# Dummy products in front of three groups, a later start for a weight conversion, and a new order of groups

## The chip, the cores and the metric

The kernel runs on one NeuronCore of a Trainium2 chip. The metric is the device time of one execution in microseconds (us); lower is better. The engines are called as the profile calls them: PE is TensorE (PEld its weight loads), DVE is VectorE, ACT is ScalarE, POOL is GpSimd, and SP issues nearly all transfers.

## What is computed

Three layers run one after another: a delta-rule attention with a 48 x 48 state for each of 4 x 8 heads over 768 tokens, a product layer, and a layer of soft routing over 32 slots.

```python
for t in range(S):                                   # 768 tokens, state 48x48 for each head
    y[:, :, t] = einsum('bhd,bhde->bhe', q[:, :, t], state)
    v_old = einsum('bhde,bhd->bhe', state, kt)       # kt: normalised key
    state = state + bt * outer(kt, vt - v_old)
x = y.transpose(0, 2, 1, 3).reshape(3072, 384)
h = ((x @ w1) * (x @ w2)) @ w3                        # 384 -> 1024 -> 1024
x = h @ w_out                                         # 1024 -> 384
logits = x @ phi                                      # 384 -> 32 slots
d = softmax(logits over tokens); c = softmax(logits over slots)
slot_in = d.T @ x
slot_out[e] = relu(slot_in[e] @ w1[e]) @ w2[e]        # 8 experts, 4 slots each
return c @ slot_out
```

The weights of the second layer (w1, w2, w3, w_out, phi) arrive as 64-bit floats and are turned into 32-bit floats on the chip.

## The kernel before

The tokens of each head are cut into 24 pieces of 32 (`chain0` to `chain23`), and two pieces make one of 12 chunks. In one piece the recurrence is a small triangular system: `G` products (line 476) give the inner products of keys and queries, `solve0` to `solve5` (lines 503 to 618, DVE and POOL) invert the triangles of four pieces at once, and the `chain` steps carry the state on. The steps of chain n are `pre` (POOL, line 644), `ks` (PE, line 658, then a subtraction on DVE), `vv` (PE, line 669, four copies on ACT), `yy` (PE, line 679, one copy on ACT), for odd n `ss` (PE, line 689, the state), and `xt` (line 701: three transposes on PE, then a copy on ACT and a subtraction on DVE). `xt` fills the tile xT of its chunk.

Once both pieces of chunk c have gone through `xt`, `prod` c runs: eight steps of 18 products of 128 x 256 (line 754), 144 for a chunk, each step with an ACT copy (line 758) and a DVE multiplication (line 763). `gtr` c turns the result around (line 771) and `post` c makes logits, softmax and the weighted sums (lines 778 to 857). The whole of w3, w_out and phi is folded into one matrix `wphi`, which `post` 0 is the first to need. So the second layer's conversions come before: `w12.0` to `w12.7` convert w1 and w2 (lines 353 to 355), and the 32 steps labelled `w3` convert w_out (eight, products on lines 370 and 375) and w3 (24, products on lines 391, 395 and 404). A step of `w3` issues a raw load on SP, six element-wise operations on DVE, ACT and POOL (lines 328 to 337), a store to DRAM on SP, and PE products with copies. Four raw tiles (`hold`) take turns.

The order is written by times. `when` and `spread` put every step in a list with a time in units of chunks, plus the `SHIFT` of its label; `spread(TW0, TW1, ...)` places the 32 steps of `w3`. `run` sorts the list and traces the steps in that order. The tile scheduler then fixes each engine's instruction order: of the instructions that it takes to be ready, the one traced first goes first. Each engine then works through its own list in order. PSUM tiles are dealt from pairs of banks by tag: `at` (chain, joins of the solves, most G products), `tr` (conversions, `gtr`, `post`) and `ab` (`prod`). `xt` of chain n takes `at` for n < `NXT` and `tr` from there on.

After the last chunk a tail computes the experts and the output. There, `warm` issues runs of eight or two 128 x 128 bf16 products into spare columns of the bank `sacc` (line 211), whose results nothing reads.

Of the kernel before, what the change touches and what calls it, by code (L numbers as in the profile page):

```python
# [11 lines left out]
BF16 = mybir.dt.bfloat16  # L12
# [30 lines left out]
DR = 0.223  # L43
NU = 2
NUG = 10
TW0 = 0.51
TW1 = 0.8
CL = 1.003
NW = 2
# [7 lines left out]
W1 = -0.8  # L57
WG = (0, 3, 7)
PV = (0, 1, 2, 3)
P0 = (-8.466, -1.081, -0.8, -0.6)  # L60
NR12 = 2
NSPLIT = 0
NXT = 12
GL = (0.35, 0.659, 0.85, 1.06)
NX = 6
NO = 8
GX = 3.912
LT = 1.693
LTS = 0.467
JAT = (1, 2, 3)  # L70
PP = 16
LAST = 1
EA = 11.832
JO = (-0.7, 0.007, 0.216)
G1 = -0.439
S1 = -0.015
S2 = 0.006

# [21 lines left out]
SB = -0.192  # L100


SHIFT = {'w3': -0.052, 'solve4': 0.109, 'gtr3': 0.007, 'solve3': 0.315, 'prod11': 0.006, 'chain20': 0.021, 'gtr8': -0.158, 'chain17': -0.056, 'gtr6': 0.158, 'post0': -0.014, 'chain19': 0.048, 'gtr10': 0.016, 'back0': 0.257, 'gtr2': -0.016, 'chain13': -0.173, 'gtr9': 0.002, 'back1': 0.128, 'post10': -0.015, 'chain23': -0.207, 'gtr0': 0.04, 'G8': 0.031, 'gtr11': -0.005, 'chain8': -0.107, 'gtr5': 0.116, 'chain5': -0.257, 'prod7': -0.026, 'chain10': -0.118, 'v6': 0.004, 'chain15': 0.036, 'prod6': 0.084, 'chain12': -0.053, 'v19': 0.5, 'G16': -0.125, 'post8': 0.057, 'prod10': 0.031, 'chain1': -0.277, 'v10': -0.038, 'chain4': 0.021, 'chain22': -0.057, 'G12': -0.152, 'prod9': -0.214, 'G22': 0.034, 'P0': -0.102, 'prod8': -0.053, 'v14': 0.146, 'solve2': 0.227, 'load7': 0.158, 'load6': -0.201, 'v13': -0.51, 'gtr1': 0.069, 'solve0': -0.184, 'post9': -0.107, 'load10': 0.047, 'G14': 0.047, 'chain18': -0.04, 'chain16': -0.002, 'chain2': -0.275, 'post4': -0.112, 'load2': -0.042, 'chain21': -0.033, 'v21': -0.195, 'chain6': 0.289, 'w12': 0.061, 'load0': 0.01, 'load1': -0.089, 'v20': -0.163}

TRACE = None

# [24 lines left out]
def kern(ctx, tc, kq, vt, kt, bl, w12, w3, wo, phi, w1e, w2e, consts, out):  # L131
    nc = tc.nc
    V, A, G, T = nc.vector, nc.scalar, nc.gpsimd, nc.tensor
# [61 lines left out]
    sv = px.tile([128, 4, H * D], F32, name="sv")  # L195
    sacc = [ps.tile([128, 512], F32, name=f"sacc{i}") for i in range(2)]
# [8 lines left out]
    zw = cs[:, C_ID:C_ID + 64].bitcast(BF16)  # L205
# [14 lines left out]
    def before(p):  # L220

        return p - 4 if p < HP else p - 5
# [19 lines left out]
    def lab(l):  # L242
        if TRACE:
            TRACE(nc, l)

    def when(t, *steps, label="when"):

        t += SHIFT.get(label.split(".")[0], 0.0)
        for f in steps:
            events.append((t, len(events), f, label))  # L250

    def spread(lo, hi, steps, label="-"):
        for i, f in enumerate(steps):
            when(lo + (hi - lo) * (i + 0.5) / len(steps), f, label=f"{label}.{i}")

    def run():
        for t, _, f, label in sorted(events, key=lambda z: z[:2]):
            lab(label)
            f()
        events.clear()  # L260
# [103 lines left out]
    def wo_steps():  # L364
        def cv(g):
            w = to_f32(raw_load(wo[:, g, :], DM, f"wo{g}"), DM, f"wo{g}")
            SP.dma_start(out=wod[:, g, :], in_=w)
            p = tr(f"wot{g}")
            for k in range(3):
                T.transpose(p[:, k * 128:(k + 1) * 128], w[:, k * 128:(k + 1) * 128], ident)  # L370
            wt = pl["stage"].tile([128, 384], F32, tag="cf", name=f"woT{g}", bufs=2)[:, 0:DM]
            A.copy(wt, p[:, 0:DM])
            p = tr(f"wm{g}")
            for k in range(3):
                T.matmul(p[:, 0:32], lhsT=wt[:, k * 128:(k + 1) * 128], rhs=phis[:, k, :], start=(k == 0), stop=(k == 2))
            V.tensor_copy(mwp[:, g, :], p[:, 0:32])

        return [lambda g=g: cv(g) for g in range(8)]
# [79 lines left out]
    def g_step(n, hs, which="gp"):  # L458

        s, n4 = divmod(n, 4)  # L460
        if n4 == 0 and "g" in which and hs[0] == 0:
            Dg[s] = pk.tile([128, 32, 32], F32, tag="L", name=f"dg{s}", bufs=NL)
        t = kl_of(n // 2)
        k = [(3, 3), (5, 1)][n % 2]

        span = {"gp": [((3, 7), (0, 4)), ((5, 7), (0, 2))], "g": [((3, 4), (3, 4)), ((5, 6), (1, 2))],
                "p": [((4, 7), (0, 3)), ((6, 7), (0, 1))]}[which][n % 2]
        nb = span[0][1] - span[0][0]
        p = (ab if n // 4 == 1 else at)(f"{which}{n}_{hs[0]}")
        gp = p[:, 0:len(hs) * nb * 32].rearrange("p (h k i) -> p h k i", h=len(hs), k=nb)  # L470
        for h in hs:
            for b in range(4):
                r, kc, j = srow(b), kcol(h, b), b // 2
                lo, hi = span[j]
                slots = slice(lo, hi) if j == 0 else slice(hi - 1, lo - 1 if lo else None, -1)
                m = T.matmul(gp[trow(n, b), h - hs[0]], lhsT=t[r, k[j], kc], rhs=t[r, slots, kc], start=True, stop=True)  # L476
        last_g[:] = [m]
        blocks = {}
        if "g" in which:
            blocks["g"] = 0  # L480
        if "p" in which:
            blocks["p"] = o = len(which) - 1
            blocks["x"] = o + 1
        g_evac(n, hs, gp, blocks, n < PP and n not in PV)

    def g_parts(p):

        h = H // 2
        return [lambda: g_step(2 * p, range(h)), lambda: g_step(2 * p, range(h, H)), lambda: g_step(2 * p + 1, range(H))]
# [145 lines left out]
    def chain_steps(n):  # L635
# [59 lines left out]
        def xt():  # L695
            ys = st["y"]
            if t2 == 0:
                xT[c] = [pl["xt"].tile([128, 3, 2, 128], F32R, tag="xT", name=f"xT{c}_{i}", bufs=4) for i in range(2)]
            p = (at if n < NXT else tr)(f"xp{n}")
            for k in range(3):  # L700
# [164 lines left out]
    def zeros(t=held4):  # L865
        V.memset(t[0:64, 5, :], 0.0)
        V.memset(t[64:128, 1, :], 0.0)

    def first():
        V.memset(sv[:, 0, :], 0.0)  # L870
        G.memset(sv[:, 1:4, :], 0.0)
        for t in kls:
            zeros(t)
        for p in sacc:
            T.matmul(p[:, 0:384], lhsT=sv[:, 0, 0:128], rhs=sv[:, 0, :], start=True, stop=False, skip_group_check=True)

    def behind0(f):

        def g():
            with tc.issue_after(ends[0].ins):  # L880
                f()
        return g

    def behind_x(f):

        def g():
            with tc.issue_after(solved[0].ins):
                f()
        return g

    def behind_w12(f, k):

        def g():
            with tc.issue_after(last_v[k].ins if k >= 0 else ends[0].ins):
                f()
        return g
# [43 lines left out]
    when(-8.87, lambda: load_kk(0), lambda: load(2), lambda: load_b(1))  # L940
    when(-8.86, lambda: load(3), gate.clear)
    when(-8.95, first)
    when(-8.95, lambda: A.activation(out=nid, in_=ident, func=AF.Copy, scale=-1.0))
    for i in range(4):
# [7 lines left out]
    for n in range(4):  # L952
        for hs in [range(H)] if n % 2 else [range(H // 2), range(H // 2, H)]:
            f = lambda n=n, hs=hs: g_step(n, hs, "p")
            when(P0[n], f if P0[n] < -8.6 else behind_x(f), label="P0")
    spread(W0, W1, [behind_w12(f, i - AHEAD) for i, f in enumerate(w12s)], "w12")
    when(-1.0, lambda: SP.dma_start(out=phis, in_=phi))
    when(-0.75, open_main)
    spread(TW0, TW1, [behind_w12(f, 7) for f in wo_steps() + w3_steps()], "w3")

    def ct(x):

        return x - CL - DR * x / NCH
# [10 lines left out]
    for p in range(3, NCH):  # L974
# [3 lines left out]
        else:  # L978
            t = ct(before(p) + 1.01) + max(0, *[SHIFT.get(f"chain{2 * before(p) + i}", 0) for i in range(2)])
        if p > 3:  # L980
            when(t, lambda p=p: load(p))
        ready[p] = HT + 0.01 if p == HP else before(p) + 1.06
    for s in range(1, NSS):
        for p in range(2 * s, 2 * s + 2):
            if s == 1:
                for i, g in enumerate(g_parts(p)):
                    when((G1, G2)[p % 2] + 0.001 * i, behind0(g), label=f"G{2 * p}")
            else:
# [11 lines left out]
    for c in range(NCH):  # L1000
        a, b, p = main_steps(c)
        spread(c, c + 1, a, f"prod{c}")

        late = LT + LTS * c
        t, w = (c + 0.25, 1.0) if late < c + 0.25 else (max(late, c + 0.7), 0.4)
# [31 lines left out]
    when(ct(2 * NSS - 2 + SB) + 0.01, early_solve, label="T.early")  # L1037
    when(GX, early_gates, label="T.early")
    when(ct(NCH - 0.1), close_att, label="close")
    eep = {}  # L1040
    for s0 in (0, 2):
        when(EA + 0.01 * s0, lambda s0=s0: eep.update(a=halves(s0)), label="T.eeA")
        for t in range(4):
            when(EA + 0.01 * s0, lambda s0=s0, t=t: expand(eep["a"], t, pl["ee"][:, s0:s0 + 2]), label="T.eeA")
    run()
    mn_stack.close()
    ws_stack.close()
# [72 lines left out]
    for hf in range(2):  # L1120
        p = ab(f"h1p{hf}")
        for f in range(8):
            q = 32 * (f % 4)
            T.matmul(p[q:q + 32], lhsT=uT[:, f % 4, f // 4, :], rhs=w3s[hf][f],
                     start=(f < 4), stop=(f >= 4), skip_group_check=True)
# [19 lines left out]
    for f in range(8):  # L1145
        q = 32 * (f % 4)
        m = T.matmul(p[q:q + 32, 0:384], lhsT=h1T[:, f, :], rhs=wos[:, f, :], start=(f < 4), stop=(f >= 4),
                     skip_group_check=True)
# [205 lines left out]
```

## Time and profile before

| what | us |
|---|---|
| median of 3 runs | 622.87 |
| lowest and highest run | 621.13, 624.06 |
| the profiled execution's own time | 618.74 |
| its span, first to last instruction | 616.9 |
| PE busy in the span | 565.4 |
| DVE, ACT, POOL busy | 393.9, 281.8, 126.8 |

The profile is of one execution. Its time is its span and 1.84 us around it, and lies 4.13 us under the median of the runs. A busy PE is not a PE at its best: the small products of the chain overlap each other, and a product takes longer in stretches where the granted clock is 0.50 (1.2 GHz) than where it is 1.00 (2.4 GHz). The mean granted clock is 0.950.

### The profile page before, as it was taken

The numbers are of one execution on the slowest core, as the hardware profiler recorded it, in microseconds if no ns is written. First come the engines' busy times: TensorE is split into PE (matmuls) and PEld (weight loads), VectorE is DVE, ScalarE is ACT, GpSimd is POOL, SyncE is SP. The second block draws the span as 40 slices with busy tenths as digits, with TensorE's granted clock in tenths as the row PEclk, the third lists the DMA queues.
The fourth block names the chain that finished last, engine by engine and source line by source line (L and its number), as shares of the span: only waits on it lengthen the run. The fifth ranks groups of instructions, "written<-read, shape, count | busy, mean of one in ns | idle before, by whom it ended". The sixth has DMA issues, their size and how long they took to land.

```text
span 616.9 us, 26156 instructions
## 1 busy us (share of the span) xinstructions
PE 565.4 (92%) x11506; PEld 461.7 (75%) x11508; DVE 393.9 (64%) x1275; ACT 281.8 (46%) x709; POOL 126.8 (21%) x191
## 2 busy tenths in 40 slices
PE   4679879997989999999989999999989999999996
PEld 3355558895767778779879897988988888885364
DVE  3998977976699649831499827987991313224124
ACT  1047874454457444554425445435544354323023
POOL 1111274342454250122300103013011000000100
PEclk9988977798799999989989999999999999999997
DMA  6974181057548622401304040312425132688818
GB/s 181 299 165 183 29 241 55 3 156 245 157 144 243 169 72 68 101 15 39 79 3 100 16 101 16 103 59 81 141 79 202 53 109 95 229 271 321 332 67 278
DMA packets 36945, 81.73 MB, mean 132 GB/s; under 512 B 4352, under 2 KB 17792, under 8 KB 35584
## 3 DMA queue, kind: packets, MB, share of 16 engines
q1 hardware_dynamic: 36576, 79.61, 42.8%
q8 instruction: 90, 1.47, 1.0%
q10 hardware_dynamic: 256, 0.46, 0.3%
q14 instruction: 23, 0.19, 0.1%
HBM read 69.57 MB, written 10.49 MB: 130 GB/s over the span
## 4 chain that ended last, share of the span: by engine, by line
PE 39%; DVE 20%; POOL 4%; issue 2%; ACT 1%; DMA 1%; POOLq 0%; ACTq 0%; DVEq 0%
PE ab L754 18%; DVE tmp L562 5%; DVE xl L565 5%; PE gp L771 2%; PE sacc L1199 2%; PE hp L1178 2%; PE gp L476 2%; PE yp L679 2%; PE vp L669 2%; PE lp L778 1%; PE sacc L689 1%; PE ks L658 1%; DVE xl L540 1%; DVE gl L503 1%; DVE gT L763 1%
## 5 line engine op out<-in xcount | busy, mean ns | idle before, releaser
L754 PE MATMUL ab<-xT,wsl 128*128 128x256 f32 x1728 | 244.8, 294 | 0.6 <-DVE gx L763 0.5
L754 PEld LDWEIGHTS ab<-xT,wsl 128*128 128x128 f32 x1728 | 220.1, 195 | 11.3 <-issue 5.6
L763 DVE TENSOR_TENSOR gT<-ab,bs 128x256 f32<-128x256 f32 x84 | 34.9, 418 | 86.5 <-ACT bs L758 85.7
L758 ACT COPY bs<-ab 128x256 f32<-128x256 f32 x96 | 35.6, 372 | 78.0 <-PE ab L754 77.3
L644 POOL TENSOR_TENSOR v<-v,nnT 128x384 f32<-128x384 f32 x24 | 21.6, 898 | 188.1 <-DMA v<-vt 90.3
L633 ACT COPY sv<-vp 32x384 f32<-32x384 f32 x96 | 45.2, 471 | 11.2 <-PE vp L669 9.5
L565 DVE TENSOR_TENSOR xl<-xl,tmp 128x84 f32<-128x84 f32 (+35 forms) x220 | 48.9, 252 | 0.8
L562 DVE TENSOR_TENSOR tmp<-xl 128x84 f32<-128x84 f32 (+35 forms) x220 | 49.1, 253 | 0.5
L476 PE MATMUL gp<-kl 48*32 48x128 f32 (+1 forms) x1152 | 39.7, 272 | 7.0 <-ACT kl L456 4.5
L337 POOL TENSOR_TENSOR hold<-hold 128x384 f32<-128x384 f32 (+1 forms) x32 | 31.9, 999 | 45.3 <-DVE hold L334 24.5
L476 PEld LDWEIGHTS gp<-kl 48*32 48x32 f32 x1152 | 28.4, 118 | 15.0 <-ACT kl L456 6.0
L772 ACT COPY gtok<-gp 128x512 f32<-128x512 f32 x48 | 28.2, 587 | 18.2 <-PE gp L771 17.4
L456 ACT COPY kl<-gp 32x256 f32<-32x256 f32 x72 | 26.2, 364 | 22.0 <-DVE kl L441 21.1
L771 PE MATMUL gp<-cs,gT 128*128 128x128 f32 x168 | 27.4, 282 | 2.9 <-DVE gT L763 2.7
L330 DVE SCALAR_TENSOR_TENSOR hold<-hold 128x384 int32<-128x384 int32 (+1 forms) x32 | 23.7, 741 | 7.5 <-ACT hold L329 6.9
L329 ACT ACTIVATE hold<-hold,cs 128x384 int32<-128x384 int32 (+1 forms) x32 | 18.5, 589 | 18.4 <-DVE hold L328 17.2
L658 PE MATMUL ks<-sv,kl 48*32 48x48 f32 (+2 forms) x1344 | 23.9, 210 | 1.7 <-issue 1.1
L669 PEld LDWEIGHTS vp<-v,w 32*32 32x32 f32 x1536 | 19.8, 108 | 7.1 <-issue 4.0
L669 PE MATMUL vp<-v,w 32*32 32x48 f32 x1536 | 24.4, 207 | 0.6 <-DVE w L618 0.6
L658 PEld LDWEIGHTS ks<-sv,kl 48*32 48x32 f32 (+2 forms) x1344 | 19.6, 111 | 6.2 <-issue 2.9
L679 PE MATMUL yp<-sv,kl 112*32 112x48 f32 (+2 forms) x1408 | 24.2, 208 | 0.0
L771 PEld LDWEIGHTS gp<-cs,gT 128*128 128x128 f32 x168 | 19.6, 143 | 5.9 <-issue 2.8
(252 smaller groups left out, 960.0 us busy)
## 6 DMA issues: line engine op xcount, KB each, us to landing
hold<-w SPq DMA_DIRECT2D x16, 384.0 KB, 3.7
v<-vt SPq DMA_DIRECT2D x24, 192.0 KB, 2.5
kk<-kt SPq DMA_DIRECT2D x12, 384.0 KB, 6.8
kl<-kq SPq DMA_DIRECT2D x9, 512.0 KB, 7.1
kl<-w1e SPq DMA_DIRECT2D x6, 768.0 KB, 5.3
unitg<-w2e SPq DMA_DIRECT2D x6, 768.0 KB, 4.6
kl<-kq SPq DMA_DIRECT2D x9, 384.0 KB, 4.9
hold<-wo SPq DMA_DIRECT2D x8, 384.0 KB, 5.9
```

Source lines behind the costliest of these rows:

```text
L337: last_m.append(E.tensor_tensor(out=w, in0=m, in1=w, op=ALU.mult))
L476: m = T.matmul(gp[trow(n, b), h - hs[0]], lhsT=t[r, k[j], kc], rhs=t[r, slots, kc], start=True, stop=True)
L562: V.tensor_tensor(out=tmp[:, 0:n, lo:hi], in0=x[:, j + 1:32, j:j + 1].to_broadcast([128, n, hi - lo]), in1=x[:, j:j + 1, lo:hi].to_broadca ...
L565: V.tensor_tensor(out=x[:, j + 1:32, lo:hi], in0=x[:, j + 1:32, lo:hi], in1=tmp[:, 0:n, lo:hi], op=ALU.add)
L633: A.copy(o, i)
L658: T.matmul(kp[o, h], lhsT=kl[r, (5, 1)[b // 2] if t2 else 3, kcol(h, b)], rhs=sv[r, b, h * D:(h + 1) * D], start=True, stop=True, tile_pos ...
L669: T.matmul(p[o, h * D:(h + 1) * D], lhsT=w[o, 8 * n4 + h, :], rhs=r[o, h, :], start=True, stop=True, tile_position=(o.start, o.start))
L679: T.matmul(p[qrow(b), h * D:(h + 1) * D], lhsT=kl[r, (6, 0)[b // 2] if t2 else (4, 2)[b // 2], kcol(h, b)], rhs=sv[r, b, h * D:(h + 1) * D ...
L754: T.matmul(o, lhsT=w[:, m, k], rhs=x[:, k], start=(n == 0), stop=(n == 8))
L758: A.copy(bs, p[:, 256:512])
L763: V.tensor_tensor(out=gt, in0=p[:, 0:256], in1=bs, op=ALU.mult)
L771: T.transpose(p[:, t * 256 + i * 128:t * 256 + (i + 1) * 128], gt[:, t * 128:(t + 1) * 128], ident)
```

## The change

It has three parts.

1. A table `FILL` names three steps: `chain5.2` (the `vv` of chain 5), `w12.7` (the eighth conversion of w1 and w2) and `prod0.2` (the third step of prod 0). In front of each, `run` traces 16, 8 and 12 products of 128 x 128 bf16 into the spare columns of `sacc[0]`. Each is tied by order alone, with no semaphore, behind the PE instruction traced just before it. One more product of zeros at the start gives these columns a value.
2. `TW0` goes from 0.51 to 0.719, so that the 32 steps of `w3` begin 0.2 chunks later in the list and end where they ended.
3. Other constants move single groups: `solve3`, `chain13`, `chain7`, `G14`, `gtr4`, `prod5`, all `gtr` and `post` after chunk 0 (`LTS`), the early load of some expert weights (`GX`), and the first P0 and G4 steps by 0.05 and 0.004. `NXT` goes from 12 to 5.

Sorted, the two lists hold the same 641 steps. The first difference is at place 110. In the old list `load_b(2)` stood after `w3.0`, the load of v for chain 4 after `w3.1`, `chain3.0` after `w3.5`, `prod0.4` after `w3.11` and `chain3.1` after `w3.14`; in the new one these five stand ahead of all of `w3`. `chain3.2` goes from after `w3.23` to after `w3.2`, and `prod0.5` from after `w3.24` to after `w3.7`. `chain3.3` and all that follows stands behind all of `w3` in both. From there the lists agree until `gtr1.0`, `chain6.1` and `chain7.0`, which are places 203 to 209.

```diff
-TW0 = 0.51
+TW0 = 0.719
-P0 = (-8.466, -1.081, -0.8, -0.6)
+P0 = (-8.516, -1.081, -0.8, -0.6)
-NXT = 12
+NXT = 5
-GX = 3.912
+GX = 3.873
-LTS = 0.467
+LTS = 0.444
-G1 = -0.439
+G1 = -0.435
...
-SHIFT = {... 'solve3': 0.315, ... 'chain13': -0.173, ... 'G14': 0.047, ...}
+SHIFT = {... 'solve3': 0.26, ... 'chain13': -0.29, ... 'G14': 0.016, ..., 'chain7': 0.052, 'gtr4': -0.15, 'prod5': 0.158}
+FILL = {'chain5.2': 4, 'w12.7': 2, 'prod0.2': 3}
...
         for t, _, f, label in sorted(events, key=lambda z: z[:2]):
+            for _ in range(4 * FILL.get(label, 0)):
+                tc.keep_in_program_order(T.matmul(sacc[0][:, 384:512], lhsT=zw, rhs=zw, start=False, stop=False,
+                                                  skip_group_check=True))
             lab(label)
             f()
...
             T.matmul(p[:, 0:384], lhsT=sv[:, 0, 0:128], rhs=sv[:, 0, :], start=True, stop=False, skip_group_check=True)
+        zero = sv[:, 0, 0:128].bitcast(BF16)
+        T.matmul(sacc[0][:, 384:512], lhsT=zero[:, 0:128], rhs=zero[:, 0:128], start=False, stop=False, skip_group_check=True)
```

## Rows read from the trace of the kernel before

**Rows 1.** The page: busy us by engine (share of the span), instructions.
```profile
PE 565.4 (92%) x11506; PEld 461.7 (75%) x11508; DVE 393.9 (64%) x1275; ACT 281.8 (46%) x709; POOL 126.8 (21%) x191
```

**Rows 2.** Stretches: from:to, length, busy us by engine, granted clock, DMA share, GB/s.
```profile
144.41:149.56 5.15, 1.15 (x58) 0.78 (x55) 3.84 (x7) 1.91 (x5) 2.03 (x2) 0.99 0.70 230
149.56:163.04 13.48, 13.48 (x217) 9.73 (x217) 9.16 (x27) 6.64 (x17) 4.96 (x6) 0.50 0.52 153
163.04:262.14 99.10, 94.21 (x2046) 76.58 (x2049) 78.45 (x253) 52.85 (x133) 35.18 (x52) 1.00 0.50 137
262.14:600.00 337.86, 329.89 (x6460) 278.00 (x6460) 178.09 (x655) 143.49 (x371) 39.47 (x79) 0.99 0.36 113
```

**Rows 3.** Two stretches for line 754 alone (PE, PEld): the products of prod.
```profile
97.60:144.41 46.81, 24.07 (x144) 21.64 (x144) 0.88 0.32 89
144.41:149.56 5.15, 0.00 (x0) 0.00 (x0) 0.99 0.70 230
```

**Rows 4.** Timeline of 136 to 151 us, all engines: start, us, what [idle before <-releaser].
```profile
136.73 0.48 ACT L682 COPY ys<-yp 128x384 f32<-128x384 f32 x1
...
144.87 0.36 DVE L328 TENSOR_SCALAR hold<-hold 128x384 int32<-128x384 int32 x1 [2.77 <-DMA hold<-w]
...
149.56 0.66 PE L391 MATMUL w3tw<-cs,hold 128*128 128x128 f32 x2 [2.49 <-ACT part L399]
...
150.49 0.90 PE L701 MATMUL xp<-cs,ys 128*128 128x128 f32 x3
```

**Rows 5.** Timeline of SP alone, 135 to 138 us: two issues.
```profile
135.16 1.82 SPq L234 DMA_DIRECT2D kl<-kq  x2
...
137.71 0.39 SPq L234 DMA_DIRECT2D hold<-w  x1
```

**Rows 6.** Timeline of 117 to 125 us, PE rows around ks of chain 3.
```profile
117.86 1.32 PE L375 MATMUL wm<-phis,woT 128*128 128x32 f32 x6
...
119.52 3.54 PE L754 MATMUL ab<-xT,wsl 128*128 128x256 f32 x18
...
123.36 0.85 PE L375 MATMUL wm<-phis,woT 128*128 128x32 f32 x6
...
124.51 0.71 PE L658 MATMUL ks<-sv,kl 112*32 112x48 f32 x46
```

**Rows 7.** Timeline of 152 to 180 us: three transposes of line 391, twice.
```profile
157.88 0.90 PE L391 MATMUL w3tw<-cs,hold 128*128 128x128 f32 x3
...
165.71 0.55 PE L391 MATMUL w3tw<-cs,hold 128*128 128x128 f32 x3
```

**Rows 8.** The tail's dummy products on line 211: all of them, then one run.
```profile
L211 PE MATMUL sacc<-cs x38: 219/219/230, 558.7 to 574.6; 128*128 128x128 bf16 x38
...
558.69 0.62 PE L211 MATMUL sacc<-cs 128*128 128x128 bf16 x8
```

**Rows 9.** Timeline of PE alone: where the three runs of dummies would stand.
```profile
75.02 0.62 PE L354 MATMUL lo<-wsl,nid 128*128 128x384 f32 x2
...
85.13 3.21 PE L476 MATMUL gp<-kl 48*32 48x128 f32 x56 [1.73 <-ACT kl L456]
...
108.21 1.08 PE L476 MATMUL gp<-kl 48*32 48x128 f32 x32
...
184.69 0.48 PE L679 MATMUL yp<-sv,kl 128*32 128x48 f32 x25
```

**Rows 10.** Other stretches with a granted clock near 0.50, columns as in rows 2.
```profile
85.30:101.20 15.90, 14.40 (x401) 12.54 (x398) 9.55 (x16) 8.98 (x25) 11.52 (x16) 0.50 0.50 157
320.50:323.60 3.10, 3.10 (x17) 3.10 (x16) 2.15 (x12) 0.95 (x2) 0.00 (x0) 0.52 0.03 5
```

**Rows 11.** PE's longest wait from 262 to 600 us: in total, times, longest.
```profile
PE ep L857 <- DVE ec L833: 1.9, 1, 1.9
```

**Rows 12.** First step of w3 after the first solve1, and the last (timelines).
```profile
121.38 0.36 DVE L328 TENSOR_SCALAR hold<-hold 128x384 int32<-128x384 int32 x1
...
218.92 0.41 PE L404 MATMUL w3tw<-cs,part 96*128 96x32 f32 x2
```

More of the change, by code (lines that the diff above doesn't have):

```diff
@@ L100 @@
 SB = -0.192
-SHIFT = {'w3': -0.052, 'solve4': 0.109, 'gtr3': 0.007, 'solve3': 0.315, 'prod11': 0.006, 'chain20': 0.021, 'gtr8': -0.158, 'chain17': -0.056, 'gtr6': 0.158, 'post0': -0.014, 'chain19': 0.048, 'gtr10': 0.016, 'back0': 0.257, 'gtr2': -0.016, 'chain13': -0.173, 'gtr9': 0.002, 'back1': 0.128, 'post10': -0.015, 'chain23': -0.207, 'gtr0': 0.04, 'G8': 0.031, 'gtr11': -0.005, 'chain8': -0.107, 'gtr5': 0.116, 'chain5': -0.257, 'prod7': -0.026, 'chain10': -0.118, 'v6': 0.004, 'chain15': 0.036, 'prod6': 0.084, 'chain12': -0.053, 'v19': 0.5, 'G16': -0.125, 'post8': 0.057, 'prod10': 0.031, 'chain1': -0.277, 'v10': -0.038, 'chain4': 0.021, 'chain22': -0.057, 'G12': -0.152, 'prod9': -0.214, 'G22': 0.034, 'P0': -0.102, 'prod8': -0.053, 'v14': 0.146, 'solve2': 0.227, 'load7': 0.158, 'load6': -0.201, 'v13': -0.51, 'gtr1': 0.069, 'solve0': -0.184, 'post9': -0.107, 'load10': 0.047, 'G14': 0.047, 'chain18': -0.04, 'chain16': -0.002, 'chain2': -0.275, 'post4': -0.112, 'load2': -0.042, 'chain21': -0.033, 'v21': -0.195, 'chain6': 0.289, 'w12': 0.061, 'load0': 0.01, 'load1': -0.089, 'v20': -0.163}
+SHIFT = {'w3': -0.052, 'solve4': 0.109, 'gtr3': 0.007, 'solve3': 0.26, 'prod11': 0.006, 'chain20': 0.021, 'gtr8': -0.158, 'chain17': -0.056, 'gtr6': 0.158, 'post0': -0.014, 'chain19': 0.048, 'gtr10': 0.016, 'back0': 0.257, 'gtr2': -0.016, 'chain13': -0.29, 'gtr9': 0.002, 'back1': 0.128, 'post10': -0.015, 'chain23': -0.207, 'gtr0': 0.04, 'G8': 0.031, 'gtr11': -0.005, 'chain8': -0.107, 'gtr5': 0.116, 'chain5': -0.257, 'prod7': -0.026, 'chain10': -0.118, 'v6': 0.004, 'chain15': 0.036, 'prod6': 0.084, 'chain12': -0.053, 'v19': 0.5, 'G16': -0.125, 'post8': 0.057, 'prod10': 0.031, 'chain1': -0.277, 'v10': -0.038, 'chain4': 0.021, 'chain22': -0.057, 'G12': -0.152, 'prod9': -0.214, 'G22': 0.034, 'P0': -0.102, 'prod8': -0.053, 'v14': 0.146, 'solve2': 0.227, 'load7': 0.158, 'load6': -0.201, 'v13': -0.51, 'gtr1': 0.069, 'solve0': -0.184, 'post9': -0.107, 'load10': 0.047, 'G14': 0.016, 'chain18': -0.04, 'chain16': -0.002, 'chain2': -0.275, 'post4': -0.112, 'load2': -0.042, 'chain21': -0.033, 'v21': -0.195, 'chain6': 0.289, 'w12': 0.061, 'load0': 0.01, 'load1': -0.089, 'v20': -0.163, 'chain7': 0.052, 'gtr4': -0.15, 'prod5': 0.158}
+FILL = {'chain5.2': 4, 'w12.7': 2, 'prod0.2': 3}
 TRACE = None
```

## The prediction

> **What bounds the kernel now.** I read the page first. PE is busy for 565.4 of 616.9 us [rows 1], the other engines far less, so PE's list of instructions sets the time wherever it is full. That share is a mean over unlike stretches, so I cut the span where the work of PE changes. From 262.14 to 600 us PE is busy for 329.89 of 337.86 us at a clock of 0.99 [rows 2]: what is late there is late to the end, and only work taken out or clock given back helps. Ahead of that, PE is full only in appearance. I looked at the products of prod, the largest item of work, by stretch [rows 3]: all 144 of chunk 0 are done by 144.41 us, and none runs in the next 5.15 us. In these PE is busy for 1.15 us, so 4.0 us are idle. In the 13.48 us behind them the granted clock is 0.50, which is the 1.2 GHz level; it fell just after the idle time [rows 2].
>
> The timeline tells what was missing. Prod 1 needs xT, which the xt of chain 3 completes. Its input, the copy of yy, began at 136.73 and took 0.48 us, so it was there at 137.21; its transposes start at 150.49, 13.3 us later [rows 4]. They stand in PE's list behind the products of a solve1 join (line 608), and those stand among transposes of w3 (lines 391 and 395). PE waits at these w3 products: the DVE step that opens their conversion had waited 2.77 us for a raw load [rows 4]. That load was issued at 137.71, behind two loads of keys issued from 135.16 [rows 5], and its data came when the DVE went on, at 144.87: 7.2 us. So this stretch is bound by PE's own order, in which a late conversion stands in front of the transposes that prod 1 lacks.
>
> **The change part by part: w3 later.** The 32 steps are not shortened: every load, store, DVE, ACT, POOL and PE instruction stays, 64 SP issues among them. On SP they move past the load of beta and that of v for chain 4; SP has issues to spare there, so I cost that at nothing; if it had not, one issue of 0.39 us [rows 5] is the price. On POOL, of those that stood ahead, they move past the pre of chain 3, on PE, DVE and ACT past ks of chain 3 and prod0.4, and 21 past its vv. In front of chain 3's last ks products stand two pieces of converted w_out: one starts at 117.86 with prod's products following at 119.52, 1.66 us, and one starts at 123.36 with ks going on at 124.51, 1.15 us [rows 6]. With the w3 steps behind ks, these 2.8 us come off chain 3. It is a permutation: the same 2.8 us of products are done later. The gain is that they then stand where PE is idle for 4.0 us [rows 2]. So of the idle time 2.8 us are filled; what is late next is the raw load, so 1.2 us stay.
>
> **The clock.** If the idle time is 1.2 instead of 4.0 us, I expect the granted clock not to fall there. What the stretch from 149.56 to 163.04 then gives back comes from rows at either level: three transposes took 0.90 us at the low clock and 0.55 us at the full one [rows 7], a ratio of 0.61. 13.48 us of busy PE [rows 2] times 0.39 is 5.3 us. The bounds are 0 (the clock falls all the same) and 5.3. I take 5.3, since the other falls of which rows stand here follow longer waits of PE than 1.2 us; this is the boldest step.
>
> **How much reaches the end.** 2.8 and 5.3 make 8.1 us at 163 us. In the next stretch PE is busy for 94.21 of 99.10 us, 95% [rows 2], and I let that share through: 7.7 us. If it is waits of DVE that end this stretch, as little as nothing gets through; if all does, 8.1.
>
> **The dummies.** The nearest rows are the same products in the tail: eight take 0.62 us, one alone 0.219 us [rows 8], so each further one takes (0.62 - 0.219) / 7 = 0.057 us. 36 make 2.1 us on a full PE at the full clock, 4.1 us at half. Where would they stand? Those of w12.7 are tied behind the last product of w12.6, at 75.02 for 0.62 us; PE then still has a wait of 1.73 us in front of its G products at 85.13 [rows 9], so these eight hide; without that cover they cost 0.5 us. Those of prod0.2 are tied behind a G product of the group at 108.21, those of chain5.2 behind the last yy product of chain 4, at 184.69 [rows 9]. There the PE goes on at once, so 28 x 0.057 = 1.6 us lie on the path. They wait for nothing but their place, but all that is traced behind them waits for them: prod's products in one case, the vv of chain 5 in the other. Below nothing they can also go: were the stretch at 0.50 from 85.30 to 101.20 [rows 10] to stay at the full clock through the eight at 75, 14.40 x 0.39 = 5.6 us would come back. They stand ten us ahead of it, so I take nothing of it. The extra product of zeros falls in the wait for the first keys: nothing.
>
> The Trainium skill, "TensorE: Matmul & The Clock Gate", section "Back-to-back issue gap", gives about 81 ns for each product of 128 columns in a stream that also loads weights. This trace disagrees, with 57 ns. By the page the 36 would cost an estimated 2.9 us instead of 2.1.
>
> **The later constants.** They reorder steps from 214 us on. PE waits little there: its longest wait is 1.9 us [rows 11], and after it the clock is at 0.52 for 3.10 us [rows 10], worth 3.10 x 0.39 = 1.2 us. So an earlier solve3 can win 1.9 + 1.2 = 3.1 us, and another gap like this one can cost as much. Moving seven xt from `at` to `tr` saves no wait that these rows show, and can make one transpose wait for a conversion to leave the bank. I take nothing for all of it, and keep +3.1 and -3.1 for the range. The moves of P0 and G4 pass no other step.
>
> **The sum.** The profiled execution took 618.74: minus 7.7, plus 1.6, is 612.6. That execution lies 4.1 us under the median of the runs, 622.87; the forecast is for the median, 622.87 - 6.1 = 616.8.
>
> **The rivals.** Everything closes: the whole 4.0 us of idle time goes, the clock gives 5.3 and the later constants 3.1, less 1.6 for the dummies: 10.8 us, 612.1. For it speaks that xt once ahead of the late conversion has no other wait in the rows; against it, that chain3.3 and later steps still stand behind all of w3 in the list.
>
> The order hardly moves: the steps of w3 that were traced early ran early because nothing else was ready, and the scheduler may lay out nearly the same lists. Then only the dummies are left, +1.6, 624.5. For it: yy, ss and xt of chain 3 keep their place behind w3. What the page says of 81 ns would make it an estimated 28 x 0.081 = 2.3 us, 625.2, in the same class.
>
> The slower side: the conversions become the bound. They run from 121.38 to 218.92 [rows 12], 27 steps of 3.6 us, and wphi and the raw tiles hang on the last. If giving way to chain 3 costs them one step, and chains 4 and 5, whose ks, vv and yy products stand among them, slide with them, the price is 3.6 us, plus 1.6: 628.1. It decides as soon as the last product of line 404 comes later than 218.92 by more than chain 3 gained, 2.8 us. For it: PE's list mixes the two up to there. Against it: POOL, DVE and ACT have room.
>
> **How the numbers follow.** I measure "same" as within 0.5%, 619.8 to 626.0, about what a measurement of this kernel can tell from no change. Forecast 0.40, everything closes 0.18, order hardly moves 0.22, conversions bound 0.20. So faster 0.58, same 0.22, slower 0.20. The range reaches down to the second case with the later constants' 3.1 us, 609, and up to the fourth, 628. Low is 609 and high 628; what lies beyond, the fourth case with another gap or a still better order, I put at 2 in 10. The forecast's own range, with the clock's and the constants' bounds, is 613 to 621.
>
> **What would show it.** In the new profile, xt of chain 3 (line 701) should start before 147 us and prod 1 with it, with less than 2 us of idle PE between the last product of prod 0 and the first of prod 1, and no clock of 0.50 from 149 to 163. Dummies on PE should total about 2 us, with no row waiting long for them. Line 404 should end near 219. If the clock still falls at 150 or line 404 ends after 222, the forecast is wrong by its boldest step or by the slower rival.

## The result, and the profile after

The kernel after takes 624.64 us (median of 20 runs, 621.58 to 633.62), the kernel before 621.43 (20 runs, 617.66 to 626.89). The ratio of the two is 1.0059, with a 95% interval of 1.0035 to 1.0084: slower by 0.6%, 3.7 us; the medians as they stand are 3.2 us apart. The time lies inside the range of the prediction; the direction was wrong. Single executions of one kernel differ by up to 2%, and the ratio leaves out one slow execution of the kernel after, of 633.62 us. So the ratios below rest on many runs, and a single profile shows where time goes in that execution, not how much on average. The profile of after is of an execution of 624.52 us, at its median; that of before lies 2.7 us under its median, so the two profiles are 5.8 us apart where the kernels are 3.7 apart. Of the 5.8 us, 2.3 lie ahead of prod 0 already (it starts at 99.93, before at 97.60): chain 0's `xt` comes at 73.52, ahead of the first dummy, and before at 71.06. In the profile of the change without its dummies it comes at 71.31, so this part is not shown to belong to the change.

The page of after, busy us by engine (answers [rows 1]):

```profile
PE 568.8 (91%) x11543; PEld 463.4 (74%) x11545; DVE 393.6 (63%) x1275; ACT 282.6 (45%) x709; POOL 125.2 (20%) x191
```

PE is busy 3.4 us longer than in [rows 1], and the span is 5.8 us longer: the rest is idle time of PE. Stretches of after, columns as in [rows 2]; the first two lie behind prod 0, the third around the last `yy` products of chain 4:

```profile
146.68:151.06 4.38, 1.20 (x55) 0.77 (x54) 1.29 (x4) 1.41 (x4) 0.40 (x1) 1.00 1.02 393
151.06:162.00 10.94, 10.94 (x154) 8.09 (x154) 9.38 (x20) 5.25 (x15) 5.88 (x6) 0.54 0.44 122
...
178.00:186.00 8.00, 5.57 (x85) 4.87 (x86) 6.06 (x15) 3.09 (x7) 2.13 (x4) 0.57 0.63 187
```

Behind prod 0 there are still 3.2 us of idle PE and then eleven at the low clock, nearly as in [rows 2]. In the third stretch the low clock is new: PE is idle for 2.4 us and the clock is 0.57, where before was idle for 2.1 us (busy 5.89 of 8.00) and ran at 1.00. The timeline of after tells what PE waited for (start, us, what [idle before <-releaser]; L706 is the xt that was L701, L759 the prod that was L754):

```profile
141.46 0.38 SPq L236 DMA_DIRECT2D hold<-w  x1
...
145.11 0.55 PE L706 MATMUL xp<-cs,ys 128*128 128x128 f32 x3
...
149.26 0.36 DVE L333 TENSOR_SCALAR hold<-hold 128x384 int32<-128x384 int32 x1 [3.34 <-DMA hold<-w]
...
151.06 0.42 PE L400 MATMUL w3tw<-w3Tw,mwp 128*32 128x128 f32 x6 [2.14 <-ACT w3Tw L398]
...
157.29 1.01 PE L759 MATMUL ab<-xT,wsl 128*128 128x256 f32 x3
```

The `xt` of chain 3 did come early, at 145.11 where [rows 4] has 150.49, and prod 1 began at 157.29 instead of 160.30. But a raw load of w3, issued at 141.46, held DVE until 149.26; ACT had the next copy to make behind it, and PE waited at a product of w3 as before, only with `xt` now done. The idle time was moved behind `xt`; it was not filled. Then comes a second long wait of PE, here for the DVE step that adds up w3's partial sums (line 407), around the dummies in front of chain 5's `vv` (L674; PE only):

```profile
180.44 0.87 PE L396 MATMUL w3tw<-cs,hold 128*128 128x128 f32 x3 [2.81 <-DVE part L407]
...
183.81 0.71 PE L261 MATMUL sacc<-cs 128*128 128x128 bf16 x5
184.31 0.85 PE L396 MATMUL w3tw<-cs,hold 128*128 128x128 f32 x3
184.96 1.28 PE L261 MATMUL sacc<-cs 128*128 128x128 bf16 x11
186.16 0.35 PE L674 MATMUL vp<-v,w 32*32 32x48 f32 x10
```

Chain 4's `yy` began 4.1 us earlier than before, chain 5's `vv` 0.9 us later (185.30 before). And the third place, the start of prod 2:

```profile
222.23 0.41 PE L400 MATMUL w3tw<-w3Tw,mwp 128*32 128x128 f32 x4
222.57 0.31 PEld L706 LDWEIGHTS xp<-cs,ys 128*128 128x128 f32 x3 [0.20 <-DVE part L407]
222.57 0.55 PE L706 MATMUL xp<-cs,ys 128*128 128x128 f32 x3
...
223.08 0.41 PE L409 MATMUL w3tw<-cs,part 96*128 96x32 f32 x2
223.16 0.48 ACT L709 CAST xT<-xp 128x384 fp32r<-128x384 f32 x1 [0.98 <-PE xp L706]
...
223.67 0.56 DVE L710 TENSOR_TENSOR xT<-xp,xT 128x384 fp32r<-128x384 f32 x1
...
225.66 0.39 PE L759 MATMUL ab<-xT,wsl 128*128 128x256 f32 x1
```

In the kernel before, prod 1, this `xt` and prod 2 began:

```profile
160.30 2.92 PE L754 MATMUL ab<-xT,wsl 128*128 128x256 f32 x12
...
198.86 0.49 PE L701 MATMUL xp<-cs,ys 128*128 128x128 f32 x3
...
219.49 0.86 PE L754 MATMUL ab<-xT,wsl 128*128 128x256 f32 x5
```

The `xt` of chain 5 is at 222.57; in the kernel before it came at 198.86. Its releaser is a DVE step of the conversions, the one that reads their product out of a bank of tag `tr`. Prod 2 needs its two copies (the ACT and DVE rows) and began at 225.66, 6.2 us later than before (219.49). From there on each prod begins 3.3 to 6.2 us later than before, and the end comes 5.8 us later.

### The profile page after: what moved, and what is told of

The parts are those of the page before. It is cut to its first block, busy times and chain, and to the rows that moved or that the text cites. A ratio compares the mean times of both kernels' runs of the same rounds, so it can differ in the third digit from the quotient of the medians.

```text
span 622.7 us, 26222 instructions
## 1 busy us (share of the span) xinstructions
PE 568.8 (91%) x11543; PEld 463.4 (74%) x11545; DVE 393.6 (63%) x1275; ACT 282.6 (45%) x709; POOL 125.2 (20%) x191
## 4 chain that ended last, share of the span: by engine, by line
PE 63%; DVE 19%; DMA 7%; POOL 3%; issue 3%; ACT 3%; SPq 0%; DVEq 0%; ACTq 0%; POOLq 0%
PE ab L759 26%; PE gp L481 4%; DMA kl<-kq 3%; PE gp L776 3%; PE vp L674 3%; PE yp L684 3%; DMA hold<-w 2%; PE ks L663 2%; PE sacc L694 2%; DVE tmp L567 2%; PE lp L783 2%; PE sacc L1206 2%; DVE xl L570 2%; PE hp L1185 2%; DMA v<-vt 2%
## 5 line engine op out<-in xcount | busy, mean ns | idle before, releaser
L759 PE MATMUL ab<-xT,wsl 128*128 128x256 f32 x1728 | 242.8, 292 | 0.8 <-DVE gx L768 0.8
L759 PEld LDWEIGHTS ab<-xT,wsl 128*128 128x128 f32 x1728 | 218.0, 193 | 11.6 <-issue 4.9
L649 POOL TENSOR_TENSOR v<-v,nnT 128x384 f32<-128x384 f32 x24 | 20.3, 848 | 200.8 <-DMA v<-vt 130.4
L570 DVE TENSOR_TENSOR xl<-xl,tmp 128x84 f32<-128x84 f32 (+35 forms) x220 | 47.3, 248 | 0.6
L481 PE MATMUL gp<-kl 48*32 48x128 f32 (+1 forms) x1152 | 38.3, 269 | 7.8 <-ACT kl L461 4.5
L335 DVE SCALAR_TENSOR_TENSOR hold<-hold 128x384 int32<-128x384 int32 (+1 forms) x32 | 21.1, 661 | 11.5 <-ACT hold L334 11.2
L674 PE MATMUL vp<-v,w 32*32 32x48 f32 x1536 | 25.6, 209 | 2.7 <-issue 1.8
L674 PEld LDWEIGHTS vp<-v,w 32*32 32x32 f32 x1536 | 20.5, 109 | 9.7 <-issue 6.0
L684 PE MATMUL yp<-sv,kl 112*32 112x48 f32 (+2 forms) x1408 | 26.8, 211 | 0.1
L684 PEld LDWEIGHTS yp<-sv,kl 112*32 112x32 f32 (+2 forms) x1408 | 20.9, 111 | 5.9 <-issue 2.2
```

Source lines behind the costliest of these rows:

```text
L570: V.tensor_tensor(out=x[:, j + 1:32, lo:hi], in0=x[:, j + 1:32, lo:hi], in1=tmp[:, 0:n, lo:hi], op=ALU.add)
L674: T.matmul(p[o, h * D:(h + 1) * D], lhsT=w[o, 8 * n4 + h, :], rhs=r[o, h, :], start=True, stop=True, tile_position=(o.start, o.start))
L684: T.matmul(p[qrow(b), h * D:(h + 1) * D], lhsT=kl[r, (6, 0)[b // 2] if t2 else (4, 2)[b // 2], kcol(h, b)], rhs=sv[r, b, h * D:(h + 1) * D ...
L759: T.matmul(o, lhsT=w[:, m, k], rhs=x[:, k], start=(n == 0), stop=(n == 8))
```

## The experiments

Ratios are to the kernel before on the same chip, with 95% intervals. Two theories stood at first: A, the later start lets the conversions become the bound, as the slower rival said; B, the later start gains, and the dummies and the later constants cost more than that. Theories O, D, C and W came later and stand in the expectations.

**w3's later start alone.**

```diff
-TW0 = 0.51
+TW0 = 0.719
```

> The kernel before with TW0 at 0.719 alone. Theory A: slower, ratio 1.003 to 1.010, with xt of chain 3 some 3 to 6 us earlier and the last product of line 404 some 4 us later, and PE waiting 2 to 3 us for a conversion near 178 us. Theory B and C: no slower, ratio 0.993 to 1.001; the forecast's own step, chain 3 ahead, would show as 0.990 to 0.995.

Measured: 618.97 us, 0.9956 (0.9926 to 0.9987). Faster, by 2.7 us: A falls for this start, and the first step of the prediction had the right sign and a third of its size. This execution (616.11 us) stands 2.6 us under that of [rows 1], close to the 2.7 us of the ratio, so its rows can be read for the size, to a microsecond or so: it begins prod 0 1.2 us later than before (98.77). PE by stretch: busy, clock, DMA share, GB/s.

```profile
140.00:144.00 4.00, 4.00 (x30) 0.57 1.02 210
144.81:149.60 4.79, 4.53 (x129) 1.00 0.92 322
149.60:152.40 2.80, 2.80 (x73) 1.00 0.37 132
152.40:154.90 2.50, 1.52 (x67) 0.83 0.71 212
154.90:158.00 3.10, 3.10 (x19) 0.50 0.53 147
158.00:161.00 3.00, 3.00 (x21) 0.52 0.78 240
161.00:164.00 3.00, 3.00 (x100) 1.00 0.40 115
```

And its timeline of PE, ahead of two falls of the clock, around the start of prod 1 and that of prod 2:

```profile
139.57 0.85 PE L375 MATMUL wm<-phis,woT 128*128 128x32 f32 x6 [0.53 <-ACT woT L372]
...
154.05 0.64 PE L404 MATMUL w3tw<-cs,part 96*128 96x32 f32 x2 [0.98 <-DVE part L402]
...
154.94 4.21 PE L754 MATMUL ab<-xT,wsl 128*128 128x256 f32 x18
...
216.72 0.41 PE L404 MATMUL w3tw<-cs,part 96*128 96x32 f32 x2
216.96 2.03 PE L754 MATMUL ab<-xT,wsl 128*128 128x256 f32 x15
...
225.84 2.42 PE L754 MATMUL ab<-xT,wsl 128*128 128x256 f32 x18 [1.15 <-DVE gT L763]
...
230.33 0.33 PE L814 MATMUL pp<-cs,pT 128*128 128x128 f32 x1 [1.62 <-ACT pT L802]
```

Between prod 0 and prod 1 (144.81 to 154.90) 1.2 us are idle, against 4.0 in [rows 2]. The clock fell all the same at 154, but for some 6.8 us instead of 13.48. It had fallen at 140 as well, behind a wait of 0.53 us, where before ran at 1.00; over the whole of 110 to 150 us both kernels have 0.91. Prod 1 begins 5.4 us earlier than before, prod 2 only 2.5, right behind the last product of the conversions (216.72, 2.2 us earlier than in [rows 12]). Behind it PE waits 1.15 us for the products' DVE step and 1.62 us for the routing of chunk 0; before had 0.58 us at the second place and nothing at the first.

**Dummies alone.** `FILL` and the zero product put into the kernel before.

> The kernel before with the three runs of dummies (and the product of zeros) alone. Theory A, the w3 conversions bind from 120 to 220 us and slide because they start later: nothing of that is here, so only the 28 dummies on the path count, +1.6 us, ratio 1.000 to 1.003, last product of line 404 at 219 +- 1.5. Theory B, the dummies and what they push aside cost it: at least the whole +3.2 us of the change, ratio 1.004 to 1.008. Theory C, the later constants cost it: as A.

Measured: 628.84, 1.0143 (1.0104 to 1.0183): dearer than either theory, and more than twice what the whole change costs.

**The later constants alone**, all of part 3 of the change.

> The kernel before with the later constants alone (NXT 5, LTS, GX, P0, G1 and the SHIFT entries). Theory C: slower, ratio 1.003 to 1.010, with xt of chain 5 some 20 us later than at 199 us. Theory A and B: ratio 0.998 to 1.002.

Measured: 624.64, 1.0055 (1.0026 to 1.0084), with chain 5's `xt` at 219.20 and prod 2 at 223.49.

**The change without its dummies**, the zero product kept.

```diff
-FILL = {'chain5.2': 4, 'w12.7': 2, 'prod0.2': 3}
+FILL = {}
```

> The changed kernel without the dummies. Theory B: at or under the kernel before, ratio 0.995 to 1.001. Theory A and C: still slower, ratio 1.002 to 1.006, only 1.6 us under the changed kernel.

Measured: 623.65, 1.0029 (0.9999 to 1.0058). So on the kernel after the dummies cost about 0.003, 1.9 us, against 0.014 with their zero product on the kernel before. The intervals with and without them overlap (1.0035 to 1.0084 and 0.9999 to 1.0058), so 0.003 is an estimate; that it is less than 0.014 is clear. The same instructions have two prices.

**NXT alone, and the change without it.** `n < NXT` decides whether the `xt` of chain n takes a bank of tag `at` or of `tr`.

```diff
-NXT = 12
+NXT = 5
```

> The kernel before with NXT at 5 alone. Theory C1: the whole loss of the later constants is here, ratio 1.003 to 1.009, xt of chain 5 near 220 us, logits of chunk 0 and prod 2 some 4 us later. Rival, the other later constants (solve3, gtr, chain13 and so on) cost it: 0.998 to 1.002.

Measured: 624.12, 1.0048 (1.0015 to 1.0082). That is nearly all of the 1.0055 of the later constants. PE in this kernel:

```profile
216.56 0.44 PE L701 MATMUL xp<-cs,ys 128*128 128x128 f32 x2
...
217.27 0.33 PE L701 MATMUL xp<-cs,ys 128*128 128x128 f32 x1
...
218.52 0.41 PE L404 MATMUL w3tw<-cs,part 96*128 96x32 f32 x2
...
220.84 2.04 PE L754 MATMUL ab<-xT,wsl 128*128 128x256 f32 x15
```

The conversions end when they did (218.52, [rows 12] 218.92), yet `xt` of chain 5 comes at 216.56 instead of 198.86 and prod 2 1.35 us later than before. This execution (620.04 us) is 1.3 us above that of [rows 1]; the rest of the 3.0 us that the runs give is not in this profile.

The kernel after with NXT back at 12:

> The changed kernel with NXT back at 12. Theory C1, the transposes of chain 5 wait for a bank of tag tr that the w3 conversions hold, and prod 2 waits for them: xt of chain 5 back from 222.6 to about 199 to 203 us, prod 2 some 4 us earlier, ratio to the kernel before 0.998 to 1.002. Theory B alone (only the dummies cost): still 1.004 to 1.008. By what the dummies alone did (1.0143) and TW0 alone (0.9956) added up: 1.006 to 1.012.

Measured: 631.49, 1.0155 (1.0101 to 1.021), the opposite of what the run above suggests: with the dummies in the kernel, `NXT` at 5 is faster by 0.0096, 6 us. The two following groups show which parts this comes with.

**Both starts without dummies and zero product**, with NXT at 5, 6 and 12 (`TW0` and all later constants).

> The kernel after without dummies and without the zero product: w3's later start and all the later constants. Beside the run of the same without dummies but with the zero product (1.003) it tells the cost of that product where it hardly moves the order (8 rows of PE, none on ACT, POOL and SP). Theory O: 1.000 to 1.005, the same as with it, since the order is the same. A cost of the product itself (a bank that it holds, a wait at the start): 0.992 to 0.998, lower by about 0.01.

> w3's later start and all the later constants, no dummies, no zero product, the transfer constant 6 instead of 5: the transposes of chain 5 stay in the bank of the norms, those of later chains go to the conversions' bank. If chain 5's transposes are the cost (they came at 219 to 222 us instead of 199 wherever the constant is 5): 0.995 to 0.999, as with 12. If the later chains' are: 1.002 to 1.006, as with 5.

> The kernel before with w3's later start and the later constants, the transfer constant left at 12, no dummies. If the parts add up: later start alone 0.9956, and the later constants' loss of 1.0055 is the 1.0048 of the transfer constant, so 0.996 to 0.998, as fast as the later start alone. If they don't (the run of after with that constant at 12 gave 1.0155): 1.004 to 1.012.

Measured: with 5, 623.09, 1.0036 (0.9999 to 1.0073); with 6, 619.73, 0.9993 (0.996 to 1.0025); with 12, 619.55, 0.9965 (0.9932 to 0.9999). Moving NXT from 5 to 12 is worth 0.007, 4.4 us. By the ratios 0.0043 of it comes with the first step, which gives chain 5's `xt` alone its old bank back, but the intervals of neighbours overlap. In the profile with 6 that `xt` is at 194.81 and prod 2 at 218.15:

```profile
194.81 0.49 PE L701 MATMUL xp<-cs,ys 128*128 128x128 f32 x3
...
217.90 0.41 PE L404 MATMUL w3tw<-cs,part 96*128 96x32 f32 x2
218.15 2.03 PE L754 MATMUL ab<-xT,wsl 128*128 128x256 f32 x15
```

With 12 the later start keeps its gain (0.9965 beside 0.9956): the other later constants are worth nothing that these runs can tell. The kernels with w3's later start alone and with all later constants but NXT beat both the kernel before and the kernel after.

**The zero product, and more or fewer dummies, on the kernel before.**

> The kernel before with the one zero product ahead of the work that the dummies need, and no dummy at all: the null of the four runs with dummies. One 128x128x128 product, 0.06 us of PE. Theory O (the loss of the dummy runs lies in the new order of all engines that any added instruction sets off, not in the dummies): ratio 1.007 to 1.014, as in the runs with 8, with 16 and with 36 dummies. Theory D (each group of dummies delays the chain that it stands in front of): 0.997 to 1.003.

> The kernel before with the eight dummies in front of w12.7 alone. If the dummies cost by the time they take on PE, this is the cheapest of the three: 0 to +0.6 us, ratio 0.999 to 1.002. If they cost because every engine's order is laid out anew, it can be as dear as the others: 1.004 to 1.010. The forecast had it hidden at 0.

> The kernel before with the 16 dummies in front of vv of chain 5 alone. By their time on PE: +0.9 us, ratio 1.000 to 1.003, with vv of chain 5 later by 1 us and all ahead of it as before. By a new order: steps long ahead of vv of chain 5 move too, ratio anywhere from 0.995 to 1.012.

> The kernel before with zero product and each group of dummies doubled: 72 instead of 36, another 2.1 to 2.6 us of PE by the dummies' own rows. Theory D (their time counts in full, or more than in full): above the 36 by 0.004 to 0.014, so 1.018 to 1.028. Theory O: the order is re-laid once and the dummies' own time is mostly hidden, 1.009 to 1.018.

| kernel before with | ratio | 95% interval |
|---|---|---|
| the zero product, no dummies | 1.0106 | 1.0071 to 1.0140 |
| and 8 dummies at w12.7 | 1.0110 | 1.0064 to 1.0156 |
| and 16 at chain5.2 | 1.0113 | 1.0075 to 1.0150 |
| and all 36 | 1.0143 | 1.0104 to 1.0183 |
| and twice 36 | 1.0164 | 1.0128 to 1.0200 |

One product of 0.06 us costs 1.1%, and the dummies behind it little more: 36 add 0.0037 (2.3 us), 72 add 0.0058 (3.6 us). The intervals of these rows overlap from one to the next. Theory D falls, as it has the zero product at nothing; O stands. What the zero product does is in the instruction lists. Counted in the two profiles, about 170 of PE's 840 runs of like products stand elsewhere or are cut otherwise (the expectations count by finer rows: 312, 41 and 8). On DVE two multiplications of prod 0 (line 763) now stand behind conversion steps that they stood ahead of, and the last starts at 155.35 instead of 149.60. In the profile prod 0 ends at 153.4 instead of 144.1, and the end of the conversions and prod 2 come 5 us late:

```profile
223.87 0.41 PE L404 MATMUL w3tw<-cs,part 96*128 96x32 f32 x2
...
224.67 1.58 PE L754 MATMUL ab<-xT,wsl 128*128 128x256 f32 x11
```

The same product added to two other kernels hardly moves a list and costs nothing that can be told: about 17 runs of like products on PE with NXT at 5 (1.0036 without it, 1.0029 with it), 42 with NXT at 12 (0.9965 without, 0.9993 with):

> The kernel after without dummies, with the zero product, the transfer constant 12. Against the run without the zero product (0.9965) it moves 41 rows of PE's order, against 312 on the kernel before. If the zero product costs by the order that it sets off: 0.994 to 1.000. If the product itself costs where the constant is 12: 1.005 to 1.012.

Measured: 619.81, 0.9993 (0.9957 to 1.0029). Beside the change without its dummies (1.0029, conversions to 221.96, prod 2 at 224.57), which differs from this kernel by `NXT` alone, this is a third measure of `NXT`: 0.0036, 2.2 us, with intervals that overlap. On this last kernel it is the dummies that re-lay the lists, about 170 runs of PE not counting their own, and they cost 0.016: the 1.0155 above. The end of the conversions and prod 2, first without the dummies:

```profile
215.80 0.41 PE L409 MATMUL w3tw<-cs,part 96*128 96x32 f32 x2
216.05 2.03 PE L759 MATMUL ab<-xT,wsl 128*128 128x256 f32 x15
```

and with them:

```profile
231.64 0.64 PE L409 MATMUL w3tw<-cs,part 96*128 96x32 f32 x2
...
232.64 1.01 PE L759 MATMUL ab<-xT,wsl 128*128 128x256 f32 x3
```

16 us lie between the two, more than the 10 us between the kernels, since the second execution (635.56 us) lies above its median and the first (616.21 us) under it; 36 dummies take 2.7 us by their rows in the second. On the kernel after, the dummies move as many runs (about 170) and cost 0.003. So the number of moved rows doesn't set the cost. It must lie in which they are; which, in each case, these runs don't tell.

**Still later starts of w3.**

```diff
-TW0 = 0.51
+TW0 = 0.80
```

> The kernel before with w3's start at 0.80, 0.29 chunks later instead of 0.21. If giving way to chain 3 has more to give: 0.988 to 0.995. If the conversions become the bound from some start on (the slower rival of the prediction): 1.000 to 1.008.

Measured: 627.69, 1.011 (1.0061 to 1.016). Here the slower rival is plain: chain 3's `xt` is at 143.05, prod 1 at 155.24, 5.1 us early, and the conversions end 4.4 us late; PE waits for them on the way, and prod 2 stands behind them:

```profile
206.32 0.82 PE L391 MATMUL w3tw<-cs,hold 128*128 128x128 f32 x3 [1.48 <-DVE part L402]
...
217.03 0.52 PE L391 MATMUL w3tw<-cs,hold 128*128 128x128 f32 x3 [1.57 <-DVE part L402]
...
223.27 0.41 PE L404 MATMUL w3tw<-cs,part 96*128 96x32 f32 x2
...
223.90 0.63 PE L754 MATMUL ab<-xT,wsl 128*128 128x256 f32 x3
```

**Shorter conversions, on the kernel before.** In fifteen profiles (before, after and thirteen of the kernels above) prod 2 begins between 216.05 and 232.64, and from there to the end of the execution it is 398.9 to 402.9 us: most of the difference lies ahead of prod 2. Does the end of the conversions set prod 2?

```diff
+            if f == 6:
+                SP.dma_start(out=w3d[:, 7, cols], in_=w)
...
+                if f == 6:
+                    V.tensor_copy(wphi[:, 7, :], p[:, 0:32])
...
-        return [lambda a=(f, j): cv(*a) for f in range(8) for j in (0, 3, 6)]
+        return [lambda a=(f, j): cv(*a) for f in range(7) for j in (0, 3, 6)]
```

> The kernel before without the last 3 of the 32 conversion steps of w_out and w3: the eighth block of w3 is taken from the seventh (stored and copied from it), so that block is left out of the computation. Theory C (the end of the conversions sets when prod 2 begins, and the rest follows): their last product comes some 8 us earlier, as far as one block is behind the other in the kernel before (210.70 to 218.92), and the time falls by 4 to 8 us, 0.987 to 0.993. Theory W (only their work on PE counts): the products left out make about 2.7 us between the starts of their rows and those behind, 0.994 to 0.998.

Measured: 622.61, 1.0046 (1.0018 to 1.0073): slower, with work left out; C and W both fall. The conversions do end 8.2 us earlier, and prod 2 begins at 215.81, but solve2's joins, 6.6 us later than before, now trail it. PE by stretch, columns as above:

```profile
212.00:220.00 8.00, 8.00 (x109) 1.00 0.14 40
220.00:230.00 10.00, 10.00 (x215) 1.00 0.24 78
230.00:245.00 15.00, 13.32 (x404) 1.00 0.18 53
```

PE is full from 212 to 230, where before waited 0.75 us at 216.33, and 1.7 us of another wait stand behind that (for the routing's `pT`, 0.58 us before). Prod 3 begins at 265.58, 0.4 us before that of the kernel before, where prod 2 had a lead of 3.7. So the end of the conversions is late in the kernels that lose, but it is one of several strands that meet between 215 and 265 us, and freeing it alone gives nothing.

## Why the prediction was wrong, step by step

**What bounds the kernel.** Right as far as it went: PE's order, with `xt` of chain 3 behind a late conversion. w3's later start alone brings `xt` and prod 1 forward and wins. What it missed is that the conversions, chain 5 and solve2 meet again before prod 2 and prod 3.

**w3 later.** Right in size: 2.8 us of idle time should go and 1.2 stay; 1.2 stay in the run of this step alone, and `xt` of chain 3 starts 2.7 us earlier (147.81). That it is again 1.2 is in part luck: the wait that stays, 0.98 us, is not for the raw load but for the DVE step of line 402. In the kernel after, 3.2 stay: with the dummies in the lists the raw load came too late again (the wait of 3.34 us above); in the profile without them 1.1 us stay.

**The clock.** This term was mis-sized. I took the upper bound, 5.3 us, on the reason that the falls of which rows stood there follow longer waits than 1.2 us. The run of this step alone shows a fall after one wait of 0.98 us, and one of three us at 140 after a wait of 0.53. The fall at 154 lasted some 6.8 us instead of 13.48, so 6.7 x 0.39 = 2.6 us came back. With the 2.8 above that is 5.4, and chain 4's first `ks` products, behind the low clock in both kernels, began 5.4 us earlier (161.49 and 166.89). Prod 1 began 5.4 us earlier too, but it stands inside the low clock in both. In two kernels without dummies the wait at the same place was shorter, 0.16 us (the zero product, NXT at 12) and 0.34 us (NXT at 6), and the clock was at 1.00 from 148 to 172; in both it had been at 0.50 for 6.8 us from about 140 on, with a wait of 0.93 and 0.94 us there. In the whole change the low stretch is 10.94 us at 0.54, and a second one of several us comes with it.

**What reaches the end.** This step failed most. I let 95% through, the busy share of PE from 163 to 262 us, which made 7.7 us of 8.1. Of the 5.4 us that were there, 2.6 reached the end. By the profile of w3's start alone, chain 5's `xt` still leads by 5.1 us (193.81), prod 2 by 2.5, the routing's product on line 814 by 0.7 (230.33), behind the two waits of 1.15 and 1.62 us for DVE and ACT, and prod 3 by 2.9 again (263.08 and 265.98), since before waits 1.19 us for DVE at 261.71. So half of the lead was gone ahead of prod 2, where the conversions end only 2.2 us earlier, and what the two waits took was given back before prod 3. A busy PE is no measure of how much of a lead passes: its list was laid out anew, and the strands that meet ahead of prod 2 didn't all come forward by as much. The prediction named that bound, "as little as nothing gets through", and gave it no weight. So w3's later start came to -2.7 instead of -7.7.

**The dummies.** Their price on PE was about right: 8 take 0.62 us again in the kernel after (57 ns for each further one, where the Trainium skill, "TensorE: Matmul & The Clock Gate", section "Back-to-back issue gap", has about 81), twelve 0.84. The sixteen take longer, 1.99 us, since they fell into the low clock. Their cost in the runs, 1.9 us on the kernel after and 2.3 on the kernel before with the zero product, is near the 1.6 of the sum; on the kernel after with NXT at 12 it is 10 us, which no time on PE explains.

```profile
77.35 0.62 PE L261 MATMUL sacc<-cs 128*128 128x128 bf16 x8
...
111.23 0.84 PE L261 MATMUL sacc<-cs 128*128 128x128 bf16 x12
```

What failed is "The extra product of zeros falls in the wait for the first keys: nothing." It is nothing that can be told in the kernels with w3's later start and the later constants, by the luck of the list that the scheduler laid out there; on the kernel before it costs 1.1%. The prediction had bounds for the time of the dummies, and none for what a new list can cost.

**The later constants.** This term was put at nothing, and without the dummies it alone takes back what w3's start gained. "Moving seven xt from `at` to `tr` ... can make one transpose wait for a conversion to leave the bank. I take nothing for all of it" names the mechanism that came and prices it at 0. In three pairs of kernels without dummies it cost 0.004 to 0.007, 2.2 to 4.4 us, about as much as w3's start gained or more. The row that the term rests on [rows 11] begins at 262 us; the loss lies ahead of that. The steps of `w3` are all traced ahead of chain 5's `xt`, so in a bank that both share it can't start before nearly all of them have left. From 198.86, twenty us ahead of prod 2, it moved to between half a us and two us ahead of the conversions' last product in every kernel with NXT at 5, and prod 2 moved behind it. The trace of before had both times, 198.86 and 218.92 [rows 12], and PE's list would have told which of the seven was first needed.

**The sum and the rivals.** w3's later start is worth -2.7 us by the runs, where the sum has -7.7. All other parts together take the ratio from 0.9956 to 1.0059, +6.4 us, where the sum has +1.6. That turned the sign. How the 6.4 divide depends on the order in which the parts are added, which a sum of separate prices leaves out. With the dummies last the ratios run 0.9956, 0.9965 (the other constants), 1.0036 (NXT), 1.0029 (the zero product), 1.0059 (the dummies): NXT costs most. With NXT last they run 0.9956, 0.9965, 0.9993, 1.0155, 1.0059: the dummies cost 10 us and NXT gives 6 back.

The slower rival's sign to look for came true, line 404 (now 409) starting 4.2 us after 218.92, at 3.7 us instead of its 5.2. But its reason was another: w3's start alone ends the conversions earlier, and with nothing else changed only a start at 0.80 makes them late. By the profiles of the two kernels that differ by NXT alone, the late end comes with NXT at 5 (221.96 and 215.80). "The order hardly moves", 624.5, has nearly the measured time, and is wrong: the order moved in every list, and the time is a difference of larger terms. Two bounds were also wrongly worked out: the low end of the range, 609, takes the 3.1 us of the later constants off 612.1, which has them already, and the forecast's own 613 to 621 leaves out its "as little as nothing", with which 622.87 + 1.6 = 624.5 is reached.

**What would show it.** `xt` of chain 3 before 147: yes, 145.11. Prod 1 with it, less than 2 us idle, no clock of 0.50 from 149 to 163: no to all three. Dummies of about 2 us: 3.45. Line 404 near 219: 223.08, past the 222 that the prediction set as its own refutation.

**What stays open.** Which of the moved instructions cost the 1.1% of the zero product on the kernel before, and the 10 us of the dummies with NXT at 12, and why such changes of the lists are nearly free elsewhere; so also why NXT at 5 costs without the dummies and gains with them; and which strand sets the time between prod 2 and prod 3 once the conversions are out of the way.

## What to carry to other kernels

A change of a buffer's tag can tie the moved step to what is traced before it under that tag: look up when its old and new neighbours run and who needs it first, before you price it at nothing. A lead at one stall counts for the end only as far as the other strands that meet PE further on are as early; follow it to the next place where PE waits for another engine. Where a scheduler lays out the lists, run a null edit first: here one product of 0.06 us moved the time by 1.1%, more than w3's later start (0.4%) or all the later constants (0.55%) did by themselves. And don't add up prices of parts that were measured in different lists.

## What the runs showed of the hardware

The granted clock fell to 0.50 after less idle time than I had expected. In the run of w3's later start alone PE was idle for 0.98 us in front of one product and for 0.21 us 4.5 us before that, and the clock was at the 1.2 GHz level for some 6.8 us from there. In the same run it was at 0.57 from 140 to 144 us, behind one wait of 0.53 us at 139.57. In two other kernels, where the wait at the first place was 0.16 and 0.34 us, it stayed at the 2.4 GHz level there (148 to 172 us). And a bank shared by tag shows in the trace as a releaser with which the waiting instruction shares no data: chain 5's transposes are released by the DVE step that reads w3's partial sums.
